# Attention into an MLP on one core: merged softmax sums, a shared product bank, early score chunks in ring banks, and a new written-out order

## The chip, the cores and the metric

The kernel runs on one core of a Trainium2 chip. A core has several engines that run their own instruction queues side by side: TensorE (PE, matrix products; its weight loads are listed as PEld), VectorE (DVE), ScalarE (ACT), GpSimd (POOL) and SyncE (SP). Matrix products land in PSUM, which has eight banks of 512 float columns for 128 partitions; everything else lives in SBUF or, outside the core, in HBM, and is moved by DMA. The metric is the device time of one execution in microseconds; lower is better. A profiled execution also gives a span, from the first instruction to the last.

## The reference

There are 8 batches of 8 heads with 576 queries and keys of 64 numbers, and 16 extra "beacon" keys in front of the keys that every query sees. The other keys are causal. The attention's output, as 4608 tokens of 512 numbers, goes through an MLP with a sigmoid gate.

```python
scores = scale * np.matmul(q, k_all.transpose(0, 1, 3, 2))
scores = np.where(causal, -1000000000.0, scores)
a = np.exp(scores - scores.max(-1, keepdims=True))
a /= a.sum(-1, keepdims=True) + 1e-09
x = np.matmul(a, v_all)        # then heads side by side: 4608 x 512
h = x @ w_in                   # 512 x 2048
g = h * (1.0 / (1.0 + np.exp(-1.702 * h)))
out = g @ w_out                # 2048 x 512
```

## The kernel before

**Attention.** The 64 (batch, head) pairs are taken as 16 sets `s` of four heads; two sets make a batch. For a set, q and k are loaded by DMAs issued on POOL (line 399), transposed on DVE in 32 x 32 blocks (`e_turn`, line 455), and the scores come from PE with keys on the partitions (`e_qk`, line 484). A head has 64 numbers, as two rows of 32, so four heads run together, each in a 32-row strip of PE's array, and each column is streamed twice. Only blocks at or below the diagonal are made: 1664 columns per head. They are cut into 55 chunks; a chunk's scores fill a PSUM tile `s` of four banks, one per head, and ACT writes exp of it into `E` (`e_exp`, line 495). There is one tile `s`, so chunk i+1 waits for the exponentials of chunk i. The diagonal blocks are masked on POOL (`e_mask`, line 516) or, for the first masks of sets 0 and 1, on DVE (line 509).

The value products and the softmax sums are one function (`e_av`, line 571). Four heads run together, each in a 32-column strip of the array. Index x = 0 and 1 are the even and odd value columns, x = 2 is a product with `ones`, the sum. Sets 0 to 3 ("early") do this in two halves of 288 queries. From set 4 on, DVE first adds the key blocks (`e_zadd`, line 534), so that the sum needs 576 columns instead of 1664; the halves are then queries 0 to 223 and 224 to 575, and each half has its own sum, in its own bank. A sum is transposed out of PSUM (`e_z1`, line 583), its reciprocal is taken (line 590) and spread back (line 594); `e_norm` (line 606) multiplies the values by it into `xT`, the MLP's input.

**MLP.** Tokens go in groups `g`: two of 256, then eight of 512. The first projection is `e_m1` (line 630). Groups 0 and 1 gate by tanh on ACT (line 644) and a product on DVE (`e_gate`, line 663); later ones by one ACT function (line 651). Groups 7 to 9 do the first projection in a Strassen scheme (line 831). The second projection is plain for groups 0 and 1 (line 675); for the others it is a Strassen scheme with seven products (`e_prod`, line 744) whose operands are sums on DVE (line 695). ACT scales product 1 out of its bank (`e_half`, line 755) and DVE adds the others (`e_join`, line 760), six operations for four quarters of the output, each stored by SP (line 767).

**Banks.** Four PSUM banks `u0` to `u3` are a ring for all of these products; a bank is free when the operations that close it are done. The other four are the tile `s`, and ring banks too once the last scores are done. PE works in three modes: full array (both projections), row strips (scores) and column strips (values and sums).

**Order.** Every operation is created with its dependencies and numbered in order of creation. `ORDER` holds, for each engine, the list of these numbers in the order in which the engine runs them; the planner (`Plan.run`) walks through the lists with assumed durations to give ring banks to operations. Engines wait for each other on the chip through semaphores; within an engine's queue nothing overtakes. Before the first scores, and once between the first two chunks, filling matmuls that nobody reads run on PE:

```python
FILL = {"qk0": ((72, 112, F16),), "qk1": ((2, 256, F32),)}
```

Of the kernel before, what the change touches and what calls it, by code (L numbers as in the profile page):

```python
# [7 lines left out]
F16 = mybir.dt.float16  # L8
# [9 lines left out]
        76, 100, 115, 118, 120, 106, 138, 141, 143, 108, 155, 111, 152, 129, 161, 158, 122, 131, 164, 167, 134, 127,  # L18
        170, 173, 176, 145, 125, 148, 150, 177, 182, 188, 191, 227, 194, 197, 232, 183, 203, 234, 200, 178, 237, 179,
        206, 258, 241, 209, 184, 263, 185, 212, 265, 213, 248, 246, 268, 214, 215, 401, 251, 253, 272, 218, 404, 275,  # L20
        244, 279, 219, 220, 407, 282, 284, 277, 221, 414, 320, 296, 304, 290, 302, 292, 300, 298, 312, 308, 294, 318,
        314, 310, 306, 316, 426, 435, 423, 343, 338, 339, 340, 433, 431, 438, 344, 345, 359, 349, 341, 464, 346, 350,
        351, 352, 354, 574, 355, 429, 360, 361, 577, 356, 362, 357, 372, 365, 583, 474, 477, 373, 366, 374, 367, 605,
        480, 484, 375, 482, 607, 368, 506, 502, 488, 492, 610, 490, 486, 498, 504, 500, 508, 514, 510, 516, 494, 496,
        512, 534, 593, 596, 535, 536, 539, 540, 550, 541, 542, 537, 742, 545, 546, 547, 548, 603, 745, 551, 552, 553,
        599, 601, 619, 622, 748, 555, 556, 557, 558, 561, 755, 625, 627, 629, 562, 563, 776, 568, 564, 569, 570, 571,
        779, 764, 767, 659, 637, 641, 657, 649, 651, 647, 661, 635, 631, 653, 805, 772, 770, 774, 643, 655, 633, 639,
        645, 679, 680, 815, 818, 700, 681, 682, 684, 701, 915, 690, 685, 686, 691, 692, 702, 918, 687, 693, 695, 703,
        696, 924, 821, 823, 697, 698, 706, 946, 825, 707, 713, 708, 709, 948, 934, 937, 714, 715, 716, 827, 951, 944,
        940, 942, 853, 831, 833, 855, 857, 851, 843, 835, 837, 847, 839, 845, 829, 849, 841, 1083, 960, 963, 875,  # L30
        876, 880, 877, 878, 881, 882, 1086, 968, 966, 970, 883, 1089, 902, 909, 903, 886, 891, 1096, 887, 888, 889,
        892, 893, 1117, 904, 894, 905, 896, 897, 1120, 898, 899, 910, 911, 1105, 1108, 1146, 912, 976, 994, 996, 972,
        978, 1000, 1002, 992, 984, 990, 986, 988, 974, 980, 982, 998, 1168, 1111, 1115, 1159, 1113, 1156, 1025, 1026,
        1020, 1027, 1171, 1021, 1022, 1028, 1023, 1031, 1177, 1032, 1033, 1164, 1166, 1162, 1199, 1034, 1036, 1047,
        1048, 1037, 1201, 1041, 1042, 1038, 1039, 1233, 1049, 1204, 1043, 1044, 1050, 1235, 1237, 1054, 1055, 1056,
        1057, 1239, 1249, 1190, 1241, 1265, 1251, 1242, 1253, 1255, 1187, 1245, 1267, 1258, 1281, 1257, 1269, 1216,
        1195, 1197, 1193, 1213, 1261, 1271, 1285, 1287, 1283, 1273, 1289, 1274, 1219, 1221, 1223, 1334, 1290, 1293,
        1277, 1357, 1335, 1313, 1318, 1314, 1336, 1315, 1319, 1316, 1320, 1321, 1373, 1324, 1325, 1337, 1326, 1329,
        1327, 1361, 1377, 1375, 1330, 1359, 1340, 1331, 1341, 1332, 1363, 1342, 1366, 1365, 1379, 1381, 1347, 1382,
        1348, 1369, 1389, 1385, 1349, 1343, 1395, 1393, 1391, 1405, 1350, 1397, 1398, 1409, 1437, 1407, 1411, 1413,  # L40
        1401, 1414, 1481, 1438, 1417, 1497, 1442, 1443, 1444, 1483, 1439, 1440, 1499, 1487, 1501, 1485, 1458, 1445,
        1459, 1460, 1489, 1513, 1490, 1448, 1453, 1449, 1450, 1451, 1454, 1503, 1455, 1493, 1505, 1461, 1456, 1464,
        1465, 1517, 1515, 1506, 1529, 1519, 1509, 1466, 1471, 1522, 1472, 1473, 1521, 1533, 1467, 1474, 1582, 1525,
        1535, 1537, 1531, 1538, 1561, 1566, 1562, 1541, 1588, 1567, 1589, 1563, 1564, 1568, 1569, 1572, 1590, 1573,
        1574, 1575, 1591, 1577, 1578, 1595, 1579, 1580, 1583, 1584, 1585, 1596, 1597, 1598,
    ],
    "ACT": [
        1, 3, 77, 79, 103, 101, 107, 109, 112, 153, 156, 130, 159, 162, 132, 165, 168, 135, 171, 174, 189, 192, 228,
        195, 198, 233, 235, 201, 204, 238, 180, 207, 259, 210, 264, 186, 266, 269, 216, 402, 405, 408, 222, 417, 415,
        297, 291, 303, 305, 301, 299, 293, 309, 321, 295, 319, 313, 315, 311, 307, 317, 436, 439, 342, 465, 468, 575,  # L50
        578, 584, 587, 606, 608, 503, 507, 489, 491, 493, 487, 499, 505, 509, 515, 517, 495, 501, 511, 497, 513, 611,
        538, 743, 746, 749, 756, 758, 777, 780, 660, 642, 638, 652, 658, 648, 650, 636, 632, 662, 654, 806, 644, 634,
        656, 640, 646, 809, 916, 683, 919, 928, 925, 947, 949, 952, 828, 832, 854, 856, 852, 858, 834, 838, 844, 840,
# [1304 lines left out]
```

## Time and profile before

| | |
|---|---|
| runs shown | 324.83 us median of 3 (324.30 to 324.98) |
| the profiled execution | 324.84 us |
| its span | 323.1 us |
| granted PE clock, mean | 0.992 |
| PE / DVE / ACT / POOL busy | 312.2 / 261.7 / 219.5 / 113.4 us |
| DMA | 28.85 MB in 58222 packets |

The page gives busy time per engine, then the span in 40 slices of about 8.1 us with each digit a busy share in tenths, the chain of work that ended last, and groups of instructions by source line. In a list of waits a row gives the engine and line that waited, what released it, the total, how often and the longest. In a timeline a row starts with its start and its length, and ends with the idle time before it. Matmuls overlap in PE's pipeline, so a block's cost is better read from one block's start to the next than from its own length.

### The profile page before, as it was taken

Reading aid. Unit: us, or ns where it says so; the run is one execution under the profiler, and the core shown is the slowest. Engines: PE = TensorE matmul, PEld = TensorE weight load, DVE = VectorE, ACT = ScalarE, POOL = GpSimd, SP = SyncE. Lnnn points to the kernel's source line nnn. Section 1 sums busy time; section 2 is a strip of 40 time slices with the busy share of each in tenths; the row PEclk is TensorE's granted clock in tenths of the full one; section 3 lists DMA queues with packets and bytes.
Section 4 is the critical chain, followed back from the end, with each engine's and each line's share of the span. In section 5 each row is a group of like instructions: output and inputs, shape, how many; then the busy total and the mean of one; then the engine's idle time right before and its main releaser. Section 6 shows DMA issues by size and latency. Waiting matters only on the chain. (4 is left out here: it accounts for less than half of the span.)

```text
span 323.1 us, 10371 instructions
## 1 busy us (share of the span) xinstructions
PE 312.2 (97%) x4508; PEld 230.0 (71%) x4508; DVE 261.7 (81%) x524; ACT 219.5 (68%) x272; POOL 113.4 (35%) x178
## 2 busy tenths in 40 slices
PE   7689999999999999999999999999999999999994
PEld 7467665644776467745878877646888888888884
DVE  4837798777987989976998889986999895585784
ACT  1676597677767686689767696768778735974830
POOL 8775478190328403871058208600221000000000
PEclk9899999999999999999999999999999999999998
DMA  7999999294423941396019908900111001101112
GB/s 124 163 200 208 206 185 184 54 97 85 123 70 66 185 73 34 53 183 89 2 36 134 189 3 80 176 28 2 37 34 65 4 32 34 67 2 36 65 67 97
DMA packets 58222, 28.85 MB, mean 89 GB/s; under 512 B 41280, under 2 KB 53568, under 8 KB 58176
## 3 DMA queue, kind: packets, MB, share of 16 engines
q0 software_dynamic: 47552, 18.49, 48.4%
q1 hardware_dynamic: 10560, 9.69, 9.3%
q8 instruction: 35, 0.57, 0.7%
q14 instruction: 11, 0.09, 0.1%
q10 hardware_dynamic: 64, 0.01, 0.0%
HBM read 37.22 MB, written 9.44 MB: 144 GB/s over the span
## 5 line engine op out<-in xcount | busy, mean ns | idle before, releaser
L495 ACT ACTIVATE E<-s 128x2048 f16<-128x2048 f32 (+5 forms) x66 | 98.9, 1515 | 41.4 <-PE s L484 40.9
L630 PE MATMUL u<-xT,w 128*128 128x256 f16 (+1 forms) x512 | 87.3, 326 | 0.6 <-ACT g L651 0.5
L516 POOL TENSOR_SCALAR_AFFINE_SELECT E<-E 128x512 f16<-128x512 f16 (+3 forms) x78 | 48.8, 658 | 107.5 <-ACT E L495 94.2
L630 PEld LDWEIGHTS <-w 128*128 128x128 f16 x512 | 49.0, 98 | 34.7 <-issue 1.9
L651 ACT ACTIVATE g<-u 128x512 f16<-128x512 f32 x80 | 43.2, 599 | 15.6 <-PE u L630 15.4
L744 PEld LDWEIGHTS <-g 128*128 128x128 f16 x512 | 48.5, 98 | 7.1 <-issue 0.3
L744 PE MATMUL u<-w,g 128*128 128x256 f16 x384 | 49.9, 273 | 0.0
L760 DVE SCALAR_TENSOR_TENSOR osb<-u,osb 128x512 f32<-128x512 f32 x56 | 37.6, 683 | 13.6 <-PE u L744 11.7
L484 PEld LDWEIGHTS <-kT 32*128 32x128 f16 x1376 | 25.6, 93 | 20.6 <-issue 12.1
L744 PEld LDWEIGHTS <-sA 128*128 128x128 f16 x384 | 36.3, 98 | 5.1 <-issue 0.3
L484 PE MATMUL s<-qT,kT 32*128 32x32 f16 (+20 forms) x1376 | 34.9, 230 | 3.9 <-ACT E L495 2.0
L859 ACT ACTIVATE g<-u 128x512 f16<-128x512 f32 x48 | 26.9, 602 | 12.4 <-PE u L831 6.8
L744 PE MATMUL u<-tB,sA 128*128 128x256 f16 x256 | 34.9, 273 | 0.1
L606 DVE TENSOR_TENSOR xT<-u,rz 128x352 f16<-128x352 f32 (+2 forms) x52 | 25.8, 518 | 7.4 <-PE u L571 7.1
L415 POOL DMA_DIRECT2D vb<-in_v_dram x32 | 27.4, 876 | 2.2 <-DMA qn<-in_q_dram 1.2
L571 PE MATMUL u<-E,vb 128*32 128x352 f16 (+8 forms) x928 | 27.9, 265 | 0.0
L534 DVE TENSOR_TENSOR zs<-zs,E 128x1344 f16<-128x1344 f16 (+2 forms) x36 | 22.6, 628 | 2.3 <-POOL E L516 1.6
L571 PEld LDWEIGHTS <-vb 128*32 128x32 f16 (+1 forms) x928 | 19.8, 97 | 5.5 <-issue 1.5
L455 DVE STREAM_TRANSPOSE kT<-kn 128x576 f32<-128x576 f32 x16 | 20.1, 1258 | 2.3 <-DMA kn<-in_k_dram 1.5
L831 PE MATMUL u<-xT,w 128*128 128x256 f16 x144 | 20.5, 273 | 0.0
L831 PEld LDWEIGHTS <-w 128*128 128x128 f16 x192 | 18.8, 98 | 2.2
L455 DVE STREAM_TRANSPOSE qT<-qn 128x576 f32<-128x576 f32 x16 | 19.9, 1241 | 0.1
(73 smaller groups left out, 397.5 us busy)
## 6 DMA issues: line engine op xcount, KB each, us to landing
out_dram<-osb SPq DMA_DIRECT2D x36, 256.0 KB, 2.3
kn<-in_k_dram POOLq DMA_DIRECT2D x16, 288.0 KB, 6.3
qn<-in_q_dram POOLq DMA_DIRECT2D x16, 288.0 KB, 6.8
vb<-in_v_dram POOLq DMA_DIRECT2D x24, 128.0 KB, 6.6
w<-in_moe_w_in_dram POOLq DMA_DIRECT2D x8, 256.0 KB, 9.6
w<-in_moe_w_out_dram POOLq DMA_DIRECT2D x4, 512.0 KB, 13.8
vb<-in_v_dram POOLq DMA_DIRECT2D x8, 112.0 KB, 5.0
vb<-in_v_dram POOLq DMA_DIRECT2D x8, 80.0 KB, 7.8
```

The costliest lines, as they stand in the source:

```text
L415: nc.gpsimd.dma_start(out=t[0 : hi - lo, j, h0:h1, :], in_=v[b, h0:h1, lo:hi, :].rearrange("h n d -> n h d"),)
L455: nc.vector.transpose(out=f32(dst.rearrange("p n e -> p (n e)")).rearrange("p (r t) -> p t r", t=TR), in_=f32(src[:, :]).rearrange("p (t c ...
L484: nc.tensor.matmul(sc[:, h, o : o + w], kT[s % NB2][r : r + 32, j * P : (j + 1) * P, d], qT[s % NB2][r : r + 32, a : a + w, d], start=(d = ...
L495: nc.scalar.activation(out=Es[s][:, :, c0:c1], in_=ss[i][:, :, o : o + c1 - c0], func=AFT.Exp, scale=0.125,)
L516: nc.gpsimd.affine_select(out=blk, in_=blk, compare_op=ALU.is_ge, fill=0.0, base=off + (Nb if j == 0 else 0), pattern=[[0, Q], [1, w]], ch ...
L571: nc.tensor.matmul(u[32 * h : 32 * h + 32, a:e], lhs, src[0:kw, h, col : col + e - a], start=first, stop=last,)
L630: nc.tensor.matmul(u[:, o + a - t0 : o + e - t0], w1t[:, kp, nt * P : (nt + 1) * P], xT[:, kp, a % XR : (e - 1) % XR + 1], start=(kp == 0) ...
L651: nc.scalar.activation(out=gts[g][:, n0:n1, 0:w], in_=rings[("m1", g, n0)][:, 0 : n * w].rearrange("p (n w) -> p n w", n=n), func=AFT.Gelu ...
L744: nc.tensor.matmul(u[:, HM * mt : HM * (mt + 1)], lhs[:, n, mt * P : (mt + 1) * P], rhs[:, n, :], start=(n == 0 and mt == 0), stop=(n == H ...
L760: nc.vector.scalar_tensor_tensor(out=osbs[(g, dst)][:, :], in0=rings[("p", g, p)][:, :], scalar=scale_of(g), in1=osbs[(g, src)][:, :], op0 ...
L831: nc.tensor.matmul(u[:, HM * n : HM * (n + 1)], lhs[x][:, (2 * i + n) * P : (2 * i + n + 1) * P], rhs[:, x, :], start=fresh and n == 0 and ...
L859: nc.scalar.activation(out=gts[g][:, n : n + 2, HM * h : HM * (h + 1)], in_=rings[src][:, :].rearrange("p (n w) -> p n w", n=2), func=AFT. ...
```

## The change

- **Merged sums.** From set 4 on, the sums of all 576 queries go into one bank of 288 columns. The sum of queries 288 to 575 is made with a weight of 16 zero and 16 one columns, that of 0 to 287 with 16 ones and 16 zeros, both into the same columns: each 32-row strip then holds the one in its upper and the other in its lower 16 rows. One transpose, one reciprocal (18 numbers) and one spread (576 wide) serve the set. The transposed sums have one buffer, `zt`, instead of two.
- **Shared product bank.** Products are made in the order 1, 2, 6, 7, 5, 4, 3. Product 3 is accumulated onto product 5 in the same bank, after DVE has read product 5 for the last quarter (`c22`); the quarter `c12` is then one addition of the bank to the earlier sum, and the addition `u4` is gone. The scaled copy of product 1 waits for three earlier joins instead of one.
- **Early chunks in ring banks.** Chunks 1 (set 1) and 2 (set 0) put their scores into the four ring banks, one head in each; ACT takes each head by its own exponential. Chunk 3 waits for chunk 0's exponentials alone. Set 1's first chunk is no longer cut into two exponentials.
- **Filling.** The two fixed fillings are replaced: ahead of each PE operation that the plan starts before 20 us, wide filling matmuls are put in for about 0.83 of the gap that the plan sees, into the ring bank that has been free longest.
- **Order.** All lists are new. The planner now keeps DVE operations that are named in `HELD` and POOL's masks from running together in the plan, and assumes 5.4 us from the end of certain loads to their users. On POOL, q0 is fetched before k0, the mask tiles are made after nine further DMA issues, two loads of the first w1 columns come earlier, and the w2 loads come after sets 0 and 1 are masked. The new PE list begins: scores 0, 3, 1, 4, 2, 5; sums of sets 0 and 1; a value product; scores 6; four value products and a sum; scores 7; four first projections.

```diff
     "PE": [
-        76, 100, 115, 118, 120, 106, 138, 141, 143, 108, 155, 111, 152, 129, 161, 158, 122, 131, 164, 167, 134, 127,
...
+        76, 119, 100, 101, 102, 103, 111, 122, 112, 113, 114, 140, 126, 149, 154, 142, 129, 133, 131, 152, 145, 163,
+        166, 169, 172, 136, 138, 156, 161, 159, 175, 178, 184, 181, 199, 238, 205, 202, 217, 243, 208, 193, 245, 211,
...
+HELD = ("s", "zadd", "xsum", "wsum", "t", "mask", "bk")
...
+                if o.port:
+                    t = max(t, held[3 - o.port])
...
+        if d.eng == "Q" and d.name[:4] in ("ldqk", "ldv1", "ldv2", "ldv3", "ldv4", "ldv5", "ldv6", "ldv7"):
+            if d.name not in ("ldqk0q", "ldqk1q", "ldqk2q", "ldqk3q"):
+                return 5400
...
+    zt = cst.tile([P, HF], F32, tag="zt", name="zt")
...
+    nc.vector.memset(ones[:, 32:48], 0.0)
...
-    FILL = {"qk0": ((72, 112, F16),), "qk1": ((2, 256, F32),)}
+    FIRST, WARM, COLS = 3800, 20000, 256
...
+    RINGED = (1, 2)
...
+        if i in RINGED:
+            ss[i] = [ring_tile(("qk", i, h)) for h in range(Q)]
...
-            if half:
-                return [[2, P, 0, S - HA, zsum[s], HA - Z0, True, True, 0]]
             return [
-                [2, P, Z0, HA, zsum[s], 0, True, True, 0],
-                [2, P, 32, Z0, E, 32, True, True, 0],
-                [2, P, 0, 32, E, 0, True, True, 0],
+                [3, P, 0, HF, zsum[s], HF - Z0, True, False, 0],
+                [2, P, Z0, HF, zsum[s], 0, False, True, 0],
+                [2, P, 32, Z0, E, 32, False, True, 0],
+                [2, P, 0, 32, E, 0, False, True, 0],
             ]
...
+                    lhs = ones[0:kw, 32:64] if x == 3 else ones[0:kw, 16:48]
...
-        u = ring_tile(("p", g, p))
+        u = ring_tile(("p", g, {3: 5}.get(p, p)))
...
-                    start=(n == 0 and mt == 0),
+                    start=(n == 0 and mt == 0 and p not in (3,)),
...
-        if i:
-            deps += [exps[(i - 1, n)] for n in range(len(CHUNKS[i - 1]))]
+        if i in RINGED:
+            key = [("qk", i, h) for h in range(Q)]
...
+        elif i:
+            k = max(x for x in range(i) if x not in RINGED)
+            deps += [x for (j, n), x in exps.items() if j == k]
...
+        prod(5)
+        c22 = join(5, "u", "b", [u3], False)
+        store(c22, "b", 1, 1)
         prod(4)
-        c21 = join(4, "u", "b", [u3])
-        store(c21, "b", 1, 0)
-        prod(5)
-        u4 = join(5, "m", "m", [u3], False)
-        c22 = join(5, "u", "u", [c21, u4])
-        store(c22, "u", 1, 1)
-        prod(3)
-        c12 = join(3, "m", "m", [u4])
+        c21 = join(4, "u", "u", [c22])
+        store(c21, "u", 1, 0)
+        prod(3, 5, [c22])
+        c12 = join(3, "m", "m", [u3], at=5)
         store(c12, "m", 0, 1)
-        ends[g] = c12
+        ends[g] = [c11, c21, c12]
...
-    idle = psu.tile([P, 512], F32, tag="u3", name="u3")
     for o in order:
-        for n, w, t in FILL.get(o.name, ()):
...
+        if o.eng == "PE" and o.start < WARM:
+            free = [(max([0] + [c.end for c in plan.closers.get(x, ())]), i) for i, x in enumerate(held)]
+            since, i = min(free)
+            n = int((2.0 if until > FIRST else 1.8) * (o.start - max(until, since + 200)) / COLS)
+            if n > 1:
+                idle = psu.tile([P, 512], F32, tag=f"u{i}", name=f"u{i}")
+                for x in [f32(scrap)] * (n // 4) + [scrap] * (n % 4):
+                    nc.tensor.matmul(idle[:, 0:COLS], x[:, 0:P], x[:, 0:COLS], start=True, stop=True)
```

## The prediction

> **What bounds the kernel now.** I read the page's busy shares and slices first, then what TensorE (PE) waits for, then its timeline at the start, the chain of work that ended last for the middle, and last the busy times by stretch.
>
> ```profile
> span 323.1 us, 10371 instructions
> PE 312.2 (97%) x4508; PEld 230.0 (71%) x4508; DVE 261.7 (81%) x524; ACT 219.5 (68%) x272; POOL 113.4 (35%) x178
> ...
> PE   7689999999999999999999999999999999999994
> ...
> PEclk9899999999999999999999999999999999999998
> ```
>
> PE is busy everywhere but in the first three slices and the last. What it waits for, in total:
>
> ```profile
> PE s L484 <- ACT E L495: 2.0, 4, 0.9
> PE u L1326 <- DVE tB L311: 1.9, 1, 1.9
> PE s L484 <- DVE qT L455: 1.6, 2, 1.4
> PE u L630 <- ACT g L651: 0.5, 1, 0.5
> PE u L571 <- DVE E L509: 0.2, 1, 0.2
> ```
>
> So no engine makes PE wait for long, and time can only come from the start, from the end, or from PE's own work being cheaper. The start, PE alone (start, length, line, count, idle before):
>
> ```profile
> 8.27 0.64 PE L484 MATMUL s<-qT,kT 32*128 32x288 f16 x24 [0.24 <-DVE qT L455]
> 11.36 0.64 PE L484 MATMUL s<-qT,kT 32*128 32x288 f16 x24 [1.39 <-DVE qT L455]
> 14.06 0.83 PE L484 MATMUL s<-qT,kT 32*128 32x288 f16 x24 [0.94 <-ACT E L495]
> 16.45 0.83 PE L484 MATMUL s<-qT,kT 32*128 32x192 f16 x24 [0.16 <-ACT E L495]
> 17.21 1.32 PE L630 MATMUL u<-xT,w 128*128 128x256 f16 x8
> ```
>
> Scores (L484) and exponentials (L495) alternate through one PSUM tile: each score chunk starts when the exponential before it is done. The middle, from the chain (start, length):
>
> ```profile
> 226.57 2.29 PE u L744 x20
> 228.86 0.59 PE s L484 x33
> ...
> 230.43 1.54 PE u L571 x56
> 231.97 0.56 PE s L484 x15
> ...
> 304.65 2.18 PE u L831 x20
> ```
>
> These give the price of changing PE's tiling. Twenty full matmuls take 2.18 us, 0.109 each, when full ones follow, and 2.29 when scores follow: leaving full mode costs 0.11. A chunk has 512 columns twice, 0.436 us at 0.109 per 256, and takes 0.59: leaving score mode costs 0.15. The 56 value matmuls have 3328 columns after division by the four heads that run together, 1.42 us, and last 1.54: leaving that mode costs 0.12.
>
> ```profile
> 8.27:21.45 13.18, 9.53 (x245) 7.28 (x244) 8.36 (x22) 8.75 (x9) 9.22 (x14) 0.87 1.56 176
> 36.24:65.46 29.22, 29.04 (x581) 17.99 (x581) 23.92 (x42) 23.58 (x22) 16.75 (x28) 1.00 1.22 146
> 65.46:318.80 253.34, 252.60 (x3372) 187.91 (x3360) 212.93 (x426) 177.44 (x231) 71.41 (x107) 1.00 0.42 69
> ```
>
> The columns are length, then busy PE, PEld, DVE, ACT, POOL, granted clock. At 65.46 group 2's first projection starts; before and after do the same work up to there, so I split the sum there.
>
> **The order after 65.46.** The numbers in the order lists count operations as they are created, so the lists can be read as names. PE changes tiling 150 times in the old list and 126 in the new. From group 2 on it is 105 and 93: leaving full mode 42 to 36, scores 36 to 35, values 27 to 22. That saves 6 x 0.11 + 1 x 0.15 + 5 x 0.12 = 1.41 us, all on the path, since PE sets the end. The bounds are 0 (each saved change returns as a wait) and 2.5 (it also loses the surplus of the blocks at 65.46, 84.77 and 205.98, which take about 0.6, 0.28 and 0.24 us more than like blocks). I take 1.4, priced from adjacent rows. The Trainium skill, in "TensorEngine Tiling (Array Packing)", Key Properties, has a change of tiling drain the engine; "TensorE: Matmul & The Clock Gate", Single matmul latency, puts a drain near 175 ns, by which these 12 would give an estimated 2.1 us. The rows above, 0.11 to 0.15, decide.
>
> **Merged sums.** For 12 sets the two transposes of sums out of PSUM (536 and 405 ns by form), two reciprocals (219, 187) and two spreads (545, 411) become one 288-wide transpose (477), one reciprocal and one 576-wide spread (about 0.27 and 0.83, carried on from the shorter rows). DVE loses 2.30 - 1.58 = 0.72 us a set, 8.6 in all. The columns on PE stay 576. Worth on the path: nothing, for PE's waits for DVE in the list above (1.9, 1.6, 0.2) all lie before 12.2 us; the sum's transposes run beside PE's products. If that cover were gone, it would be worth up to the 8.6.
>
> **Shared product bank.** One join (683 ns) goes in each of 8 groups, 5.5 us of DVE, hidden likewise. Product 3 now waits until the join for c22 has read product 5. Behind it in PE's queue stand only later products; in the last group nothing else can fill. There product 7's end is followed by two joins, 2 x 0.69 plus about 0.45 of handing over, 1.83 us, against 16 matmuls of product 4, 1.75: +0.1 us, between 0 and 0.3. The very last join and store follow product 3 as before: last matmul 319.06, join until 319.82, end 323.1. Stores only change places on SP, which is idle there.
>
> **The start.** New order on PE: qk0, qk3, qk1, qk4, qk2, qk5, sums and values of the first halves with qk6 among them, qk7, then four projections. Step by step with the rows' durations:
> - q0 is fetched and transposed ahead of k0; the 0.21 us transpose of beacon keys, done while DVE waited at 3.87, now stands after q0's: qk0 at 8.47, exponentials 9.18 to 11.12.
> - qk3 (the tile is free): exponential 11.8 to 13.25 (turnaround 0.69, 1.45 each). Chunk 1 lies in four ring banks, four exponentials of 512 columns, 0.60 + 3 x 0.49 (two tanh take 1.08): 15.25. Chunk 4 to 16.6. Chunk 2 needs all four ring banks, which the first of its exponentials returns at about 16.95.
> - So the first sum starts at 17.1, was 12.16. DVE then does 2 x (0.48 + 0.21 + 0.48), about 2.4 with gaps, and four multiplications of 0.41: the last ends at 21.95, was 17.66.
> - By then PE has done all eight chunks instead of four, and seven sums or values instead of six.
>
> What is left on PE from there to group 2: 32 projection or product pieces of 0.873 (27.9), twelve chunks (10752 columns, 4.6), sums and values (15744 columns, 6.7), 29 changes (12 full, 11 scores, 6 values: 3.7): 42.9 us, to 64.85. Followed bank by bank through DVE's list to about 36 us (gates 0.65, transposes 1.25, sums as above), PE waits about 0.35 us more: 65.2, or 0.25 earlier than now.
>
> The moves on POOL: the mask tiles go behind nine more DMA issues (0.55 to 0.87 each), from 4.65 to about 12; masks are first needed by the sum at 17.1. The first w2 load goes from 17.5 to about 24.5, behind the last early masks; landing took 13.8 in the median, so 38.3, and its product starts near 38: 0 to 0.9 of wait. I take 0, since a megabyte less stands ahead of it. The filling matmuls stand in gaps of the plan and cost nothing where the gap is real; each of the wide float ones is about 0.5 us (2 took 1.13), so one in a false gap costs that. Ends for the start: 1.0 us gained (no waits, first projection 0.4 earlier) and 3.1 lost (below).
>
> **Sum.** -1.41 - 0.25 + 0.1 = -1.56 on the profiled execution's 324.84 (span 323.1 and 1.74 around it; the median of the runs is 324.83, so the same): 323.3 us.
>
> **Rivals.**
> - A, as summed: 323.3, own range 322.3 to 324.2. 42%.
> - B, the start and the surplus both come out at their good ends: -1.0 - 2.5, 321.3. For it: those blocks wait for other engines. Against: I see no step that frees them. 15%.
> - C, no change: saved changes of tiling return as short waits for the same buffers, and the change does not do what it says: 324.2 to 325.5, 10%. For it: a PE with fewer gaps meets its producers sooner. Against: almost nothing makes PE wait now.
> - C', the first projections run on a slow clock, because PE has only some 4.6 us of work from 8.5 to 22. Two blocks of eight 256-wide matmuls at 17.21 and 19.32 were busy 1.32 and 1.05 us, against 0.87, with clock 0.87 and 0.92. Four such pieces would lose 0.7 to 1.8 us: 324.0 to 325.1, 5%. The Trainium skill, "TensorE: Matmul & The Clock Gate", Part 1, speaks for it: an idle window halves the clock until PE has been busy again. By that rule the trace agrees: the first filling matmuls took 86 ns for 112 columns, against 48 at 0.109 per 256.
> - D, slower: DVE becomes the bound of the start. It has to finish about 41.8 us (gates 10.5, turning q and k of four sets 10.8, sums 9.4, multiplications 7.1, rest 4.0) between 17.56 and group 2, 88% of the time. It reached 82% in 36.24 to 65.46 and 97% at its best (24.38 of 25 us). At 82% group 2 starts at 68.55, 3.1 late: 326.6. It decides from a loss of 1.3 at the start on, that is below 85%. For it: early gates now queue behind turning q2 and the second-half sums. Against: when PE was the limit, DVE had no reason to do more. 28%.
>
> Faster by over 0.2% (about what can be told from no change): B and nearly all of A, 55%. Within: 15%. Slower: D and a little of C and C', 30%. The range from 320.8 (B and half a microsecond of error in the start) to 326.6 (D) leaves out some two in ten.
>
> **What would show it.** Right: 93 changes of tiling after group 2's start, that stretch 251.9 to 252.2 us long, DVE near 247 us busy, first projection near 22. Wrong: DVE idle before group 2 while PE waits for ring banks; score rows waiting for filling; new PE waits for joins (L760). If group 2 starts after 67 us, D has happened; if well before 64.5, my chain through DVE's list is wrong.

## The result and the profile after

The changed kernel takes 323.19 us, the median of 13 runs (322.85 to 324.39), and the kernel before 324.83 us in 13 runs beside it (324.3 to 325.49). The ratio is 0.9953, with a 95% interval of 0.9943 to 0.9964: half a per cent faster. The profiled execution shown here took 323.13 us, 1.71 less than the one that the prediction was worked out on.

The page of the changed kernel, busy times first and then TensorE's rows of the 40 slices:

```profile
span 321.4 us, 10238 instructions
...
PE 310.9 (97%) x4465; PEld 230.0 (72%) x4465; DVE 245.7 (76%) x481; ACT 219.9 (68%) x277; POOL 112.7 (35%) x178
...
PE   7779999999999999999999999999999999999995
...
PEclk9999999999999999999999999999999999999999
```

DVE lost 16.0 us of work (261.7 to 245.7) and PE 1.3 us; the span fell by 1.7. PE's share is still 97%. What PE waits for, in total:

```profile
PE u L1377 <- DVE tB L328: 2.0, 1, 2.0
PE s L506 <- ACT E L517: 1.9, 2, 1.1
PE u L655 <- issue: 0.5, 1, 0.5
PE s L506 <- DVE kT L473: 0.5, 1, 0.5
PE u L506 <- ACT E L517: 0.4, 1, 0.4
PE u L597 <- DMA vb<-in_v_dram: 0.4, 1, 0.4
PE u L597 <- POOL E L538: 0.4, 1, 0.4
PE u L597 <- DVE zt L607: 0.3, 1, 0.3
```

No row names a join (L785), so product 3's new wait for c22 does not show, and all of them lie before 26 us, the one for `issue` last. The start, PE alone:

```profile
8.93 0.64 PE L506 MATMUL s<-qT,kT 32*128 32x288 f16 x24 [0.49 <-DVE kT L473]
...
17.51 0.71 PE L597 MATMUL u<-E,ones 128*32 128x288 f16 x24
18.52 0.31 PE L597 MATMUL u<-E,vb 128*32 128x288 f16 x4 [0.30 <-DVE zt L607]
19.21 0.28 PE L597 MATMUL u<-E,vb 128*32 128x176 f16 x8 [0.39 <-DMA vb<-in_v_dram]
...
22.21 1.05 PE L655 MATMUL u<-xT,w 128*128 128x256 f16 x5
```

The first scores start at 8.93, the first sum at 17.51 and the first projection at 22.21, each 0.3 to 0.5 us later than forecast (8.47, 17.1, 21.95). The middle, from the chain of work that ended last:

```profile
222.66 2.29 PE u L769 x20
...
225.52 2.12 PE u L597 x76
...
228.23 2.73 PE u L769 x24
```

Products, values and products again, in longer pieces than before, at the same prices: twenty matmuls ahead of scores take 2.29 us as they did. Busy times by stretch (length, then PE, PEld, DVE, ACT, POOL, granted clock; the last two numbers are the DMA's and are not used here):

```profile
8.93:22.21 13.28, 9.78 (x315) 7.61 (x316) 7.85 (x20) 11.02 (x14) 10.92 (x20) 1.00 1.45 173
22.21:37.34 15.13, 14.54 (x233) 11.66 (x220) 14.48 (x30) 8.99 (x13) 8.52 (x14) 1.00 1.34 200
...
66.11:317.34 251.23, 251.10 (x3361) 188.38 (x3359) 199.36 (x381) 177.50 (x230) 67.19 (x101) 1.00 0.41 65
```

The last row is the stretch from group 2's first projection to the start of the last matmul. It is 2.10 us shorter than before (253.33 by the same two rows), with DVE down by 13.6 us in it and PE by 1.5. So the difference of the two profiled executions, which the rest of this text takes apart, is:

| part | before | after | difference |
|---|---|---|---|
| up to group 2's first projection | 65.46 | 66.11 | +0.65 |
| from there to the last matmul's start | 253.33 | 251.23 | -2.10 |
| from the last matmul's start to the span's end | 4.34 | 4.08 | -0.26 |
| sum, the span | 323.13 | 321.42 | -1.71 |
| the executions' own times | 324.84 | 323.13 | -1.71 |

In the middle stretch the blocks can be priced as in the prediction, each block's cost above 0.109 us per 256 columns: full mode 5.38 before and 4.06 after (42 and 36 blocks), values and sums 3.67 and 2.90 (27 and 22), scores 5.03 and 5.02 (35 each). That is where the 2.10 lie. By these blocks the middle has 104 changes of tiling before and 93 after: eleven fewer, not twelve. 0.46 of the full mode's 1.32 is a single block, the first one of the stretch, which took 14.57 us before and 14.10 after.

### The profile page after: what moved, and what is told of

It is laid out like the page before. It is cut to its first block, busy times and chain, and to the rows that moved or that the text cites. A ratio compares the mean times of both kernels' runs of the same rounds, so it can differ in the third digit from the quotient of the medians.

```text
span 321.4 us, 10238 instructions
## 1 busy us (share of the span) xinstructions
PE 310.9 (97%) x4465; PEld 230.0 (72%) x4465; DVE 245.7 (76%) x481; ACT 219.9 (68%) x277; POOL 112.7 (35%) x178
## 4 chain that ended last, share of the span: by engine, by line
PE 91%; DMA 3%; POOL 3%; ACT 1%; issue 1%; DVE 0%; POOLq 0%
PE u L769 31%; PE u L655 26%; PE u L856 11%; PE u L597 10%; PE s L506 8%; PE u L700 5%; DMA w<-in_moe_w_in_dram 3%; POOL w L439 1%; ACT E L517 1%; POOL vb L433 1%; POOL kn L417 0%; ACT L676 0%; POOL qn L417 0%; POOL E L538 0%; DVE xT L631 0%
## 5 line engine op out<-in xcount | busy, mean ns | idle before, releaser
L517 ACT ACTIVATE E<-s 128x2048 f16<-128x2048 f32 (+5 forms) x63 | 95.6, 1532 | 41.4 <-PE s L506 37.7
L538 POOL TENSOR_SCALAR_AFFINE_SELECT E<-E 128x512 f16<-128x512 f16 (+3 forms) x78 | 48.1, 634 | 91.4 <-ACT E L517 91.3
L785 DVE SCALAR_TENSOR_TENSOR osb<-u,osb 128x512 f32<-128x512 f32 x48 | 32.9, 685 | 22.8 <-PE u L769 18.2
L506 PEld LDWEIGHTS <-kT 32*128 32x128 f16 x1376 | 24.6, 92 | 19.7 <-issue 12.8
L506 PE MATMUL s<-qT,kT 32*128 32x32 f16 (+20 forms) x1328 | 33.1, 228 | 2.4 <-ACT E L517 1.9
L769 PE MATMUL u<-tB,sA 128*128 128x256 f16 x256 | 34.2, 273 | 0.0
L556 DVE TENSOR_TENSOR zs<-zs,E 128x1344 f16<-128x1344 f16 (+2 forms) x36 | 21.6, 601 | 1.1
```

Source lines behind the costliest of these rows:

```text
L506: nc.tensor.matmul(ss[i][h][:, o : o + w], kT[s % NB2][r : r + 32, j * P : (j + 1) * P, d], qT[s % NB2][r : r + 32, a : a + w, d], start=( ...
L517: nc.scalar.activation(out=Es[s][:, :, c0:c1] if h is None else Es[s][:, h, c0:c1], in_=sall[i][:, :, o : o + c1 - c0] if h is None else s ...
L538: nc.gpsimd.affine_select(out=blk, in_=blk, compare_op=ALU.is_ge, fill=0.0, base=off + (Nb if j == 0 else 0), pattern=[[0, Q], [1, w]], ch ...
L769: nc.tensor.matmul(u[:, HM * mt : HM * (mt + 1)], lhs[:, n, mt * P : (mt + 1) * P], rhs[:, n, :], start=(n == 0 and mt == 0 and p not in ( ...
L785: nc.vector.scalar_tensor_tensor(out=osbs[(g, dst)][:, :], in0=rings[("p", g, p)][:, :], scalar=scale_of(g), in1=osbs[(g, src)][:, :], op0 ...
```

## The experiments

The theory was the prediction's: fewer changes of tiling shorten the middle, the start is worth little, the relief of DVE is worth nothing. Times are medians, ratios are to the kernel before as run beside each. The three columns in the middle are those of the table above, from each one's profiled execution.

| kernel | us | ratio, 95% | up to group 2 | middle | end | tiling changes in the middle | DVE busy |
|---|---|---|---|---|---|---|---|
| before | 324.83 | 1 | 65.46 | 253.33 | 4.34 | 104 | 261.7 |
| after | 323.19 | 0.9953 [0.9943, 0.9964] | 66.11 | 251.23 | 4.08 | 93 | 245.7 |
| old start | 323.31 | 0.9953 [0.9941, 0.9965] | 65.82 | 251.69 | 4.08 | 93 | |
| new start alone | 325.11 | 1.0003 [0.9994, 1.0012] | 66.24 | 252.89 | 4.34 | 104 | |
| six swaps | 324.71 | 0.9990 [0.9980, 0.9999] | 65.84 | 252.72 | 4.08 | 105 | |
| merged sums alone | 324.40 | 0.9979 [0.9969, 0.9990] | 65.99 | 252.89 | 4.34 | 101 | 253.9 |
| DVE's work back | 327.40 | 1.0080 [1.0067, 1.0092] | 65.69 | 255.44 | 4.08 | 93 | 259.9 |
| sums' work back | 325.80 | 1.0024 [1.0014, 1.0034] | 66.12 | 253.81 | 4.08 | 93 | 254.1 |
| work off the chain | 325.26 | 1.0012 [1.0002, 1.0021] | 65.30 | 253.04 | 4.08 | 93 | 259.0 |
| masks early | 323.13 | 0.9939 [0.9925, 0.9953] | 66.14 | 251.25 | 4.08 | 93 | |
| no filling in gaps | 323.22 | 0.9948 [0.9928, 0.9968] | 65.77 | 251.23 | 4.08 | 93 | |
| k first | 323.25 | 0.9945 [0.9931, 0.9959] | 66.68 | 251.24 | 4.09 | 93 | |
| first loads | 323.73 | 0.9959 [0.9946, 0.9972] | 65.99 | 251.24 | 4.08 | 93 | |
| three fewer | 324.63 | 0.9981 [0.9969, 0.9993] | 66.58 | 252.38 | 4.08 | 90 | |

Five of these kernels differ from each other in the start alone (after, masks early, no filling in gaps, k first, first loads), and their middles are 251.23 to 251.25 us. So hundredths of a microsecond can be read from this column, but not from the one ahead of it, as the next part shows.

### The start and the rest, each alone

The first kernel keeps the new code and the new order from group 2 on, but has the old filling, the old order up to group 2 and no chunks in ring banks. The second has the old code and order from group 2 on, behind the new start.

```diff
-    RINGED = (1, 2)
+    RINGED = ()
...
+    FILL = {"qk0": ((72, 112, F16),), "qk1": ((2, 256, F32),)}
```

> The changed kernel with the start of the one before: up to group 2's first projection all lists, the chunks' tiles and the filling are the old ones; from there on the new order, merged sums and shared bank. Theory (the gain lies from group 2 on, the new start costs 0.65 us: that projection at 66.11 against 65.46): projection at 65.46 +- 0.2, then 255.3 us as in the changed kernel: span 320.8, time 322.5 (322.3 to 322.8), 0.6 below the changed kernel. Rival (the new start pays for itself later, because DVE and ACT are further ahead): the stretch from group 2 on is longer than 255.3 by about what the start gains, time 323.2 or more.

> The mirror: the new start (early chunks in ring banks, new filling, new lists up to group 2), from there on the old order with two sums a set and a bank of its own for product 3. Theory: projection at 66.1, then the old 257.6 us: span 323.75, time 325.5 (325.2 to 325.8), slower than before by 0.2 percent. Rival (the start is where the gain begins): 323.9 or less.

Measured: 323.31 with the old start, as the changed kernel, and 325.11 with the new start alone, as the kernel before. The middle of both, by stretch:

```profile
65.82:317.51 251.69, 251.11 (x3371) 188.42 (x3360) 199.19 (x382) 177.81 (x231) 69.59 (x103) 1.00 0.42 68
```

```profile
66.24:319.13 252.89, 252.59 (x3360) 187.85 (x3359) 214.24 (x425) 177.18 (x230) 70.65 (x104) 1.00 0.40 64
```

The first fence is the old start, the second the new start alone. With the start held fixed the new rest shortens the middle by 253.33 - 251.69 = 1.64 us, or 252.89 - 251.23 = 1.66. With the rest held fixed the new start shortens the middle by 253.33 - 252.89 = 0.44 or 251.69 - 251.23 = 0.46. That is the middle's first block, first with the old start, then in the changed kernel:

```profile
65.82 3.63 PE L656 MATMUL u<-xT,w 128*128 128x512 f16 x16
69.94 10.52 PE L656 MATMUL u<-xT,w 128*128 128x512 f16 x48 [0.49 <-ACT g L677]
```

```profile
66.11 14.17 PE L655 MATMUL u<-xT,w 128*128 128x512 f16 x64
```

Its 64 matmuls wait 0.49 us for ACT with the old start (the prediction's list of waits has this one, at L651), and do not with the new one. What the new start does ahead of group 2 can't be told from single profiled executions. Six kernels have the same new start up to there (after, new start alone, six swaps, DVE's work back, sums' work back, work off the chain), and group 2 begins at 65.30 to 66.24 in them, 65.88 on average; in the three with the old start at 65.46 to 65.99, 65.76 on average. By these means the start is worth some -0.3 us; by the medians it is -0.1 with the new rest and +0.1 with the old one. None of this is clear of nothing. The gain that can be told lies from group 2 on, and my theory of the first run, that the start costs 0.65, was wrong: 0.65 is within what the same start differs by. Its rival, a start that pays for itself behind group 2, fits with the 0.46.

### The price of a change of tiling

Six pairs of neighbours in the new PE list are swapped, each so that two blocks become four: 12 changes more, with the same work.

```diff
-        440, 438, 357, 360,
+        440, 357, 438, 360,
...
-        1094, 1090, 1003, 1004,
+        1094, 1003, 1090, 1004,
```

> The changed kernel with six places of the order after group 2's start altered: where two value products stand side by side before a piece of the second projection, that piece goes between them. Twelve changes of tiling more (138 instead of 126), the same work. Theory (0.11 for leaving full mode, 0.12 for leaving values): 6 x 0.23 = 1.4 us more, 324.6 (324.2 to 325.0). By the Trainium skill (TensorE: Matmul & The Clock Gate, Single matmul latency) at an estimated 0.175 us each: 2.1 us more, 325.3. Rival (saved changes were worth nothing, other waits went): 323.2 to 323.6.

The middle of this kernel, by stretch:

```profile
65.84:318.56 252.72, 252.59 (x3360) 188.16 (x3359) 198.67 (x381) 177.53 (x230) 67.81 (x101) 1.00 0.41 65
```

It is 252.72 - 251.23 = 1.49 us longer with the same DVE work, 0.124 us for each change; PE is busy all through it. 0.18 of the 1.49 is one block at 191.97, which costs 0.32 above its columns instead of 0.14, so that the other changes come to 0.11 each. The prediction's prices (0.11 to 0.15) give 1.4 for these twelve. The Trainium skill, "TensorE: Matmul & The Clock Gate", Single matmul latency, has a drain of about 175 ns; one for each of the twelve would give an estimated 2.1 us. The measurement decides for the smaller price.

Three changes fewer than the new order has were tried too, on top of the kernel "first loads" below, by moving score and value blocks next to their like:

```diff
-        484, 379, 486,
+        379, 484, 486,
...
-        624, 556, 557, 622,
+        624, 622, 556, 557,
```

> The run before this one, with three places of the order from group 2 on altered so that a value product stands beside others: a piece of product 4 ahead of the values of set 5, one value product behind score chunk 31, one beside its neighbours after chunk 32. 123 changes of tiling instead of 126. Theory (0.124 us a change, as twelve more cost 1.49): 0.37 less than that run, 322.3. Rival (the value products then wait for ring banks): no gain or a loss up to 0.5 us.

Its median is 0.9 us above that of the kernel it was made from, not 0.37 below. Five of its twelve executions took no more than 323.82 us, close to the 323.73 of that kernel, so the loss is not in every one of them; the profiled one took 324.76. PE's timeline at one of the moved blocks, first the changed kernel, then this one:

```profile
97.50 1.32 PE L597 MATMUL u<-E,vb 128*32 128x352 f16 x40
98.76 0.64 PE L506 MATMUL s<-qT,kT 32*128 32x448 f16 x16
```

```profile
97.56 1.04 PE L599 MATMUL u<-E,vb 128*32 128x224 f16 x36
98.77 0.75 PE L599 MATMUL u<-E,vb 128*32 128x352 f16 x20 [0.16 <-DVE xT L633]
99.45 0.63 PE L508 MATMUL s<-qT,kT 32*128 32x448 f16 x16
```

Here 16 value matmuls came before the stretch in the changed kernel and stand inside it now. The second half waits for a bank that DVE's multiplication (L633) has to free, and the scores start at 99.45 instead of 98.76; 0.47 of these 0.69 us it had brought along from the start. At another place scores wait for exponentials:

```profile
126.73 0.66 PE L508 MATMUL s<-qT,kT 32*128 32x336 f16 x24 [0.57 <-ACT E L519]
```

Four blocks around these places, at 97.56, 124.68, 127.32 and 130.95, cost 0.38 to 0.75 us above their columns, where like ones cost 0.11 to 0.13. That is 1.5 us in all, against 0.37 that the three changes save. This is rival C of the prediction, one step further along; no gain is to be seen in that direction.

### What the relief of DVE is worth

The prediction gave DVE's 14 us less of work no value. Three kernels take the relief back without moving an operation of PE, and one gives it to the old order. First, every sum from set 4 on is transposed twice and inverted twice, and one join in each of eight groups is done twice; the repeats write the same numbers again.

```diff
-        nc.vector.transpose(out=zt[:, :], ...)
+        for _ in range(2 if s >= EARLY else 1):
+            nc.vector.transpose(out=zt[:, :], ...)
...
+        for _ in range(2 if dst == "b" else 1):
+            nc.vector.scalar_tensor_tensor(out=osbs[(g, dst)][:, :], ...)
```

> The changed kernel with DVE's saved work given back: from set 4 on the transpose of the sums and the reciprocal are done twice (12 x 0.75 us), and the join for the last quarter twice (8 x 0.69): about 14.5 us more on DVE, nothing else. Theory (DVE's relief is worth nothing on the path): 323.2, at most 323.5; DVE busy about 260. Rival (the relief pays for the gain): at least half of it is lost, 324.0 or more, and PE shows new waits for joins or multiplications.

It took 327.40 us, 2.4 us more than the kernel before, so "nothing" does not hold for the new order: DVE work of the relief's size, put back like this, costs it more than the whole gain. The middle by stretch, and one place in it, DVE's timeline and then PE's:

```profile
65.69:321.13 255.44, 253.03 (x3361) 189.17 (x3359) 213.92 (x413) 177.86 (x230) 68.73 (x101) 1.00 0.40 65
```

```profile
120.56 1.00 DVE L608 STREAM_TRANSPOSE zt<-u 128x288 f32<-128x288 f32 x2
121.60 0.57 DVE L615 RECIPROCAL rc<-zt 128x18 f32<-128x18 f32 x2
...
123.54 1.47 DVE L788 SCALAR_TENSOR_TENSOR osb<-u,osb 128x512 f32<-128x512 f32 x2
124.92 2.14 DVE L556 TENSOR_TENSOR zs<-zs,E 128x1344 f16<-128x1344 f16 x3
...
127.62 1.00 DVE L608 STREAM_TRANSPOSE zt<-u 128x288 f32<-128x288 f32 x2
```

```profile
126.04 0.65 PE L506 MATMUL s<-qT,kT 32*128 32x336 f16 x24
127.12 0.38 PE L597 MATMUL u<-zs,ones 128*32 128x288 f16 x8 [0.43 <-DVE zs L556]
...
128.68 1.05 PE L771 MATMUL u<-w,g 128*128 128x256 f16 x8 [0.26 <-DVE zt L608]
```

In the changed kernel the same stretch of DVE's queue is:

```profile
120.61 0.48 DVE L607 STREAM_TRANSPOSE zt<-u 128x288 f32<-128x288 f32 x1
...
122.77 1.47 DVE L785 SCALAR_TENSOR_TENSOR osb<-u,osb 128x512 f32<-128x512 f32 x2
124.15 1.97 DVE L556 TENSOR_TENSOR zs<-zs,E 128x1344 f16<-128x1344 f16 x3
```

The two joins there (L788, L785 in the changed kernel) stand in both. The doubled transpose and reciprocal of an earlier sum push them and the addition of key blocks (L556) back by 0.77 us, and the sum on PE waits 0.43 us for that addition; then its own doubled transpose (L608) holds its bank, and a product waits 0.26. In the changed kernel the same sum starts at 126.67 and the product at 127.90, with no wait. So the first wait comes from a place in DVE's queue, the second from a longer chain. DVE is busy for 84% of this middle, 79% of that of the changed kernel, and still PE loses 4.2 us in 255: an average says nothing of such places.

How much of that is the work itself, and how much its place in the chain from a sum to its bank? Two further kernels: the sums' repeats without the join, and about the same amount of DVE work as the first placed behind the chain, into a tile that nobody reads.

```diff
+        if s >= EARLY and done_norms.count(s) == 3:
+            for _ in range(2):
+                nc.vector.transpose(out=dum[:, :], in_=zs[(s, 0)][:, 0:224])
...
+        if (src, dst) == ("m", "m") and p == 5:
+            nc.vector.scalar_tensor_tensor(out=dum[:, :].bitcast(F16), ...)
```

> The changed kernel with only the transpose of the sums and the reciprocal done twice from set 4 on (12 x 0.75 us on DVE), the joins as they are. If the 4.2 us come from the sums' chain: 326 or more. If from the join ahead of product 3 in the shared bank: 323.2 to 324.2. If they go by DVE time alone: 9.0 of 14.5, 325.8.

> About as much work on DVE as in the run that gave DVE its work back (12 x 0.81 + 8 x 0.6 = 14.5 us, into a tile that nobody reads), but behind the last multiplication of a set and behind the last join of a group instead of inside the chains sum, transpose, reciprocal, and product 5, join, product 3. Theory now (the 4.2 us came from the longer chains: banks of the sums held longer, product 3 later): most of it goes, 323.2 to 324.6. Rival (the new order has no room for the work on DVE, wherever it stands): 326 or more.

The middle of the one with the sums' repeats and of the one with work off the chain:

```profile
66.12:319.93 253.81, 252.33 (x3361) 189.04 (x3359) 207.78 (x405) 177.63 (x230) 68.18 (x101) 1.00 0.40 65
```

```profile
65.30:318.34 253.04, 251.58 (x3360) 188.49 (x3359) 212.02 (x412) 177.51 (x230) 69.34 (x101) 1.00 0.41 65
```

The sums' repeats, 8.4 us of DVE work, lengthen the middle by 2.58 us; their trace has the same two waits of 0.43 and 0.26, where no join is doubled. The joins make the rest of the 4.21, 1.63. Off the chain 13.3 us lengthen the middle by 1.81, most of it at two places, where a projection waits for a bank that a late join frees and another for late exponentials:

```profile
203.56 1.02 PE L662 MATMUL u<-xT,w 128*128 128x512 f16 x4 [0.51 <-DVE osb L792]
240.56 1.47 PE L868 MATMUL u<-xT,w 128*128 128x256 f16 x12 [0.63 <-ACT E L518]
```

By the medians the two kernels cost 2.6 and 2.1 us. For the first, 325.80 is the number set down for a loss that goes by DVE time alone, which this run by itself can't tell from the chain; the second's 325.26 lies between its theory and its rival. Together they show that the place matters: about three tenths of a microsecond was lost for each one put into a sum's chain, and a seventh for each one behind it. These are averages over a few places, not rates, and work out of the way is not free either.

The last kernel of this part gives the old code and the old order merged sums, and nothing else of the change.

```diff
-            if half:
-                return [[2, P, 0, S - HA, zsum[s], HA - Z0, True, True, 0]]
             return [
+                [3, P, 0, HF, zsum[s], HF - Z0, True, False, 0],
+                [2, P, Z0, HF, zsum[s], 0, False, True, 0],
```

> The kernel before with the merged sums alone: old order, with one sum a set in the place of the later of the two (of the earlier for the last two sets). Theory (relief of DVE is hidden, the columns on PE stay): 324.8, between 324.4 and 325.1; DVE busy down by about 8.6 us. Rival (a freed bank and a relieved DVE let PE run without its remaining waits): 324.0 or less.

Its middle, by stretch:

```profile
65.99:318.88 252.89, 252.13 (x3372) 188.30 (x3360) 204.81 (x390) 177.35 (x231) 72.64 (x107) 1.00 0.43 69
```

With 8 us less on DVE the middle of the old order is 0.44 us shorter, and three changes of tiling that go with the merged sums' second visits are worth 0.37 of that at 0.124. That leaves about 0.1 us for the relief; the medians, 0.6 us apart, leave some 0.2. In the old order, then, the relief is worth little, as the prediction had it. It is the new order that needs it; that its fewer, longer blocks on PE ask more of DVE at once is my reading of the places shown, not a measurement. No run has the new order with two sums a set or with a bank for product 3 alone. The repeats are not the same as that work, so what the new order would do without the relief itself is not shown.

### The start's parts

Four kernels change the start alone. In the first the mask tiles are made right behind the first four loads on POOL again (16 in the list), in the second k0 is fetched and transposed ahead of q0, in the third the filling matmuls stand ahead of the first scores only, and the fourth has the first two edits and the load of the beacon values (17) right behind the mask tiles.

```diff
-        10, 8, 12, 14, 19, 35, ..., 39, 16, 33,
+        10, 8, 12, 14, 16, 19, 35, ..., 39, 33,
```

```diff
-        10, 8, 12,
+        8, 10, 12,
```

```diff
-        if o.eng == "PE" and o.start < WARM:
+        if o.eng == "PE" and o.start < WARM and until == FIRST:
```

```diff
-        10, 8, 12, 14, 19, 35, ..., 27, 17, 23, 21, 39, 16, 33,
+        8, 10, 12, 14, 16, 17, 19, 35, ..., 27, 23, 21, 39, 33,
```

> The changed kernel with one thing moved: the two mask tiles are made in fifth place on POOL again, right after the first four loads. In the changed kernel DVE waits 1.15 us for them, at 12.85. Theory (masks are not needed before the first sum; the later v load lets q0 land earlier, as k0 did at 5.5 before): first scores 0.3 to 0.5 us earlier than 8.93, first projection as much earlier, time 322.8 (322.6 to 323.2). Rival (the arrival of the first loads does not depend on the load behind them, and the value products wait for v instead): 323.2 to 323.6, first scores at 8.9.

> The changed kernel with k0 loaded and transposed ahead of q0 again, as before; nothing else is moved. Theory: the small transpose of beacon keys (0.2 us) goes back into DVE's wait: first scores 0.2 us earlier than 8.93, time 323.0 (322.8 to 323.2). Rival (which of the two lands first is what made the first landing 0.5 us later): first scores at 8.3, time 322.5.

> The changed kernel with filling matmuls ahead of the first scores alone; none in the later gaps. Theory (the clock drops in a PE with little work): granted clock below 0.9 between 9 and 22 us, the first projections at 1.1 us and more for eight matmuls instead of 0.88; 0.5 to 1.5 us more, 323.7 to 324.7. Rival (filling only delays real work by false gaps): first projection 0.2 to 0.5 us earlier, 322.8 to 323.1.

> The changed kernel with the first six things on POOL as before: k0, q0, k1, q1, mask tiles, beacon v; then its own list; k0 transposed before q0. Moving the masks alone, and k0 alone, each left the first scores at 8.9 to 9.0; with the old lists they start at 8.2 to 8.3. Theory (the small beacon load in fifth place instead of the v load is what lets the second tensor land by 6.9 instead of 7.6): first scores at 8.3, time 322.6 (322.4 to 323.0). Rival (the heavy w1 loads behind are the cause): first scores at 8.8 or later, 323.1.

Masks early: 323.13; k first: 323.25. Neither moves the first scores by more than 0.05 us (8.92 and 8.98), since the transpose of the second tensor starts at 7.61 or 7.67 whichever it is, and neither moves the time, though the first projection starts at 22.79 and 22.95. No filling in gaps: 323.22, and this is the clean look at rival C'. Its stretches from the first scores to the first projection, and just behind that:

```profile
8.61:22.26 13.65, 8.57 (x301) 6.79 (x301) 8.07 (x20) 11.12 (x14) 10.94 (x20) 0.75 1.44 174
22.26:26.20 3.94, 3.84 (x48) 3.05 (x38) 3.83 (x9) 3.13 (x4) 2.08 (x4) 1.00 1.44 198
```

Without the filling the granted clock is 0.75 in the first stretch, where the changed kernel has 1.00. That the clock falls when PE idles is as the Trainium skill has it ("TensorE: Matmul & The Clock Gate", Part 1). But the first projection starts at 22.26, against 22.21, and the clock is 1.00 from there on, so the projections do not pay for it, and the scores on the slow clock wait for exponentials either way. The filling is worth nothing here, and costs nothing.

First loads: 323.73. PE's timeline, and two stretches of it:

```profile
8.42 0.64 PE L508 MATMUL s<-qT,kT 32*128 32x288 f16 x24 [0.87 <-DVE qT L475]
...
19.02 0.28 PE L599 MATMUL u<-E,vb 128*32 128x176 f16 x8 [0.70 <-DMA vb<-in_v_dram]
...
22.97 1.26 PE L657 MATMUL u<-xT,w 128*128 128x256 f16 x10
```

```profile
20.00:21.00 1.00, 1.00 (x24) 0.71 (x28) 0.41 (x1) 0.95 (x1) 1.00 (x2) 0.50 1.19 215
...
23.00:25.00 2.00, 2.00 (x27) 1.79 (x20) 1.94 (x4) 1.87 (x3) 0.54 (x1) 1.00 1.65 183
```

The scores do start half a microsecond earlier, as the second tensor's transpose starts at 7.11 instead of 7.61. But v's load ends at about 19.0, as in the changed kernel (19.21), so the value product waits 0.70 us instead of 0.39; and then the granted clock is 0.50 from 20 to 21 and the first projection starts at 22.97, 0.76 late. This is C' in the start. What sets the clock off is not shown: it is 0.50 from 19 to 21 with masks early too, where the same product waits 0.22, and 1.00 with k first, where it waits 0.84. Group 2 starts at 65.99 all the same; the clock is 1.00 again from 23 on, and DVE is 96% busy in the changed kernel from 22 to 37, which may be why. So half a microsecond won at the head of the start, and 0.8 lost at the first projection, can't be seen at group 2, within the 0.9 us by which the same start differs. Of the four expected times only that of masks early was met, and the earlier first scores that it rested on did not come. No kernel that was run beats the changed one by more than its interval.

## Why the prediction was right, and which step was not

323.3 was forecast and 323.19 measured, case A. That they meet within 0.1 us is in part luck: the order gave 0.2 more than its term, the end 0.26 that had no term, and the start nothing that can be told, where 0.25 was put.

- **The order after 65.46.** Forecast -1.41 from 12 changes of tiling; the middle fell by 1.64 to 1.66 with the start held fixed, and twelve changes put back cost 1.49. The mechanism is shown, and its price was sized well. The count was one too high: the saved change out of a score block is the one into the projection at 65.46, ahead of the stretch, so that 6 x 0.11 + 5 x 0.12 = 1.26 was to be had. By kind, leaving full mode was forecast at -0.66 and is -1.32, of which 0.46, put at 0.6, is the first block's and belongs to the start; leaving value mode was -0.60 and is -0.77; the score blocks were -0.15 and are -0.01. What goes beyond 1.26 is surplus, of which the lower bound of 2.5 took in three blocks, at 65.46, 84.77 and 205.98. These three are gone. But others have come: behind the first block, before has blocks that are dearer than like ones by 0.78 us in all, the changed kernel by 0.43, at 105.05, 120.10, 136.33 and 171.26.
- **DVE's relief, merged sums and dropped join.** This is the step that failed. "Worth on the path: nothing" was read off the waits of the old order, and holds there, to some 0.1 or 0.2 us. For the new order it does not: 8.4 us put back into the sums' chain cost 2.58, with the joins 4.21, and 13.3 us out of the way 1.81. The sum came out right because it priced the new order with the relief in place, and gave all to the tiling changes; by these runs DVE work of the relief's size costs the new order more than these changes give. The sentence "If that cover were gone, it would be worth up to the 8.6" named the right quantity, but I took the cover for a property of the kernel, when it is one of the order.
- **Product 3's wait.** Forecast +0.1; no wait for a join appears in the changed kernel. With the join doubled, product 3 of the last group waited 0.49 us, as a join lasts 0.69: some 0.2 us of room was there, where I had worked out a lack of 0.1.
- **The start.** Forecast -0.25; -0.3 by the stretches and -0.1 to +0.1 by the medians, which is not clear of nothing. The way to it was another: group 2 did not start 0.25 earlier, but 0.1 later on average, and 0.45 came back in the first block behind it. The steps up to the first projection were 0.3 to 0.5 late from the first one on: the first transpose waited for its load until 6.07 instead of 5.60 and the second, k0's, until 7.61, steps that the forecast did not have. The first w2 product, put at 0 to 0.9 of wait, had none in the list.
- **The end.** -0.26 was not forecast. The last store landed 2.13 us after its issue instead of 2.36, and the store before it stands further ahead (1.75 us instead of 0.6). Both come with the new order in every run with it; that the distance to the other store is the cause is not shown.
- **The rivals.** D put 41.8 us on DVE between 17.56 and group 2. It did 37.32 in that stretch, 77% of the 48.55 us, and 96% (14.48 of 15.13) where it was behind, from 22.21 to 37.34; group 2 was not held up by 1.3 us, the point from which D decides. C, saved changes that return as waits, is not in this order, but it is what happens to the next three. C' happens in the start, with a clock of 0.75 without filling in gaps and of 0.50 to 0.69 from 19 to 23 us with the first loads moved, but the projections behind it ran at 1.00 from 22.26 and 23 on, and group 2 came no later. The clocks of 0.87 and 0.92 that the prediction sets beside two blocks are means of 8 to 16 and of 16 to 24 us; both blocks lie in the second. Of B, the three surpluses went, but others took the place of half of them, and the start's good end did not come. DVE near 247 and 251.9 to 252.2 us from group 2 on were named as signs; 245.7 and 251.23 were seen, the middle shorter by its first block.

## What to carry to other kernels

A written-out order and the slack it runs on are one thing: the value of taking work off an engine that nobody waits for can't be read from the waits of the old order, because a tighter order may spend it; price it by giving the work back to the new order, at more than one place in its queue. On PE count the blocks, not only the columns: a change of tiling cost 0.11 to 0.15 us here by the mode that was left, until further merges of blocks came back as waits for banks and exponentials. Count them from the start of a block to the start of the next, inside the stretch that the sum prices. Compare the parts of a start only at the point where the next stage takes over: half a microsecond won or lost before 23 us was not to be seen at 66, where the same start differed by 0.9.

## What the runs showed of the hardware that was not expected

- A granted clock of 0.75 over 13.65 us of the start did not cost time: the first block behind it ran at 1.00 and the time was 323.22 us, against 323.19. With the first loads moved the clock was 0.50 from 20 to 22 us, behind PE's wait of 0.70 us that ended at 19.02, and 1.00 again from 23 on.
- The landing of the first loads depended on what is queued around them: the transpose of the second of k0 and q0 could start at 7.61 and 7.67 us in the two orders, and at 7.11 where k0 came first and the mask tiles and a 16 KB load stood between these loads and the first load of v, so that this was issued at 5.20 instead of 3.56. With the mask tiles alone between them, and v issued at 4.66, it was 7.61 again; which of the differences decides is not shown.
- DVE was busy for 79% of the middle, and the other fifth was not all free to be used: 13.3 us of work that nobody waits for, put behind the sums and joins, took PE 1.81 us.
